# Moving the last block's transposes from crossbar DMA to TensorE, and ordering the last down group by column halves

## The chip, the cores and the metric

The kernel runs on one core of a Trainium2 chip. The metric is the device time of one execution in microseconds (us). Executions of the same kernel here agree within about 0.5%. The stage called "turn" below repeats to about 0.03 us between kernels that have the same instructions there (4.29 to 4.32 us), the "tail" only to about 0.2 us (3.53 to 3.77 us).

In profile lines, PE is TensorE's matmuls and PEld its weight loads, ACT is ScalarE, DVE is VectorE, and SPq is the queue that issues DMAs. A crossbar DMA is here a DMA with `transpose=True`, which transposes on the way.

## The reference, cut to what matters

A state-space convolution with a residual gives `h` (2048 rows of 640). Then a gated MLP is added to it:

```python
g = jnp.einsum("bsd,df->bsf", x, w_gate)      # x = layernorm(h), 640 -> 1728
u = jnp.einsum("bsd,df->bsf", x, w_up)
h = _sigmoid(g) * u
return jnp.einsum("bsf,fd->bsd", h, w_down)   # 1728 -> 640
```

## The kernel before

It works on four blocks of 512 rows. For each block, `prep` writes the normalized rows `ln2`, `turn` transposes them into `lnT`, the gate/up part makes `hm` and the down part multiplies `hm` with `Wd`. Since 1728 is 13 x 128 + 64, the last contraction step has only 64 rows; its matmuls are called half-height. A block's down part has two groups (`lp` = 0 and 2) of two 128-row sets (`k` = 0, 1). The next block's `prep` and `turn` are placed inside the down part of the present one. `DT` says per block whether `turn` uses the crossbar DMA; before, only the last block does.

```python
"DT": (0, 0, 0, 1)
# ... cut ...
def turn(b):
    ln2 = lns[b]
    lnT = lnTs[b] = xp.tile([P, 5, 4, 128], BF16, name="lnT", tag="G")
    if AT["DT"][b]:
        for i in range(4):
            nc.sync.dma_start(lnT[:, :, i, :], ln2[:, i, :], transpose=True)
        return
    # ... cut ...
    for dc in range(5):
        pt = psg_p.tile([P, 4, 128], BF16, name="ml_pt", tag="ml_pg")      # two buffers, shared with the gate
        for i in range(4):
            nc.tensor.transpose(pt[:, i, :], ln2[:, i, 128 * dc:128 * dc + 128], ident[:])
        if dc % 2 or b:
            nc.scalar.copy(lnT[:, dc], pt[:])
        else:
            nc.vector.tensor_copy(lnT[:, dc], pt[:])
# ... cut: gate/up ...
for lp in (0, 2):
    po = [[t[:, c] for c in range(2)] for t in (pso_p.tile([P, 2, 512], F32, name="ml_po", tag="ml_po") for _ in range(2))]

    def chunks(k, start, stop):
        lr = lp + k
        for ft in range(FT):                      # FT = 13
            for c in range(2):                    # column halves of 320
                nc.tensor.matmul(po[k][c][:, 0:320], lhsT=hm[:, ft, 128 * lr:128 * lr + 128], rhs=Wd[:, ft, 320 * c:320 * c + 320],
                                 start=(start and ft == 0), stop=(stop and ft == FT - 1))

    if not lp and b < NB - 1:
        prep(b + 1)
    chunks(0, True, False)
    if lp and b < NB - 1:
        turn(b + 1)
    # ... cut: four half-height matmuls, first k = 0 then k = 1 of each column half ...
    chunks(1, False, True)
    for k in range(2):
        # ... cut ...
        for c in range(2):
            if b < NB - 1:
                tb = Wd[:, 14 + k, 320 * c:320 * c + 320]
                nc.scalar.copy(tb, po[k][c][:, 0:320])
            nc.vector.tensor_tensor(h2[:, c], tb if b < NB - 1 else po[k][c][:, 0:320], h2[:, c], ALU.add)
        if b == NB - 1:
            nc.sync.dma_start(oh[b, :, lr:lr + 1, :], hs[b][:, lr:lr + 1, :])
```

## Time and profile before

| | before |
|---|---|
| median of 3 runs | 356.66 us (356.56 to 356.86) |
| span of the profiled run | 355.0 us |
| TensorE busy | 320.4 us, 90% |
| first half-height matmul of the last turn to the first gate matmul of block 3 | 302.71 to 307.01: 4.30 us |
| that gate to the first add after the last matmul | 307.01 to 351.44: 44.43 us |
| that add to the end of the span | 351.44 to 355.0: 3.56 us |

The last three rows cut the end of the kernel into the turn, the stretch that nothing in the change touches, and the tail. Their borders are start times in the timeline. The lines behind them stand in the prediction.

### The profile page before, as it was taken

How to read it: one execution, taken by the hardware profiler on the slowest of the kernel's cores; microseconds unless marked ns; L12 is line 12 of the kernel's file. 1: busy time of each engine (PE TensorE's matmuls, PEld its weight loads, DVE VectorE, ACT ScalarE, POOL GpSimd, SP SyncE). 2: the span in 40 equal slices, each digit the busy share in tenths (PEclk: the TensorE clock that was granted, in tenths of full speed). 3: DMA queues.
4: the chain of work that ended last, by engine and by line, in shares of the span. 5: the costliest groups of instructions: out<-in, count | busy, mean ns of one | idle time of the engine just before them, and what ended most of it. 6: DMA issues, size and time to landing. Idle time of an engine off the chain costs nothing.

```text
span 355.0 us, 6617 instructions
## 1 busy us (share of the span) xinstructions
PE 320.4 (90%) x2584; PEld 204.0 (57%) x2584; DVE 283.3 (80%) x570; ACT 245.9 (69%) x455; POOL 11.4 (3%) x20
## 2 busy tenths in 40 slices
PE   2587989997799999899999899998899999999995
PEld 1464667765487778755456554555554456544463
DVE  3899999999898799879999899999899951211222
ACT  6999999998999764673767845547844678455500
POOL 1020002200000000100000100000100001000000
PEclk9998999999999999999999999999999999999999
DMA  6990000454205339989500053000012000400011
GB/s 172 323 404 4 15 2 2 113 179 157 76 3 160 137 88 352 289 273 280 227 4 0 5 179 113 3 0 0 3 74 76 0 1 11 133 7 1 0 37 38
DMA packets 32391, 35.00 MB, mean 99 GB/s; under 512 B 19676, under 2 KB 27741, under 8 KB 32104
## 3 DMA queue, kind: packets, MB, share of 16 engines
q1 hardware_dynamic: 32360, 34.59, 30.7%
q8 instruction: 20, 0.33, 0.4%
q14 instruction: 11, 0.09, 0.1%
HBM read 24.70 MB, written 9.21 MB: 96 GB/s over the span
## 4 chain that ended last, share of the span: by engine, by line
DVE 28%; PE 18%; issue 14%; ACT 2%; POOL 1%; POOLq 0%; DVEq 0%; ACTq 0%
DVE u L694 5%; PE ml_po L942 5%; DVE u L693 5%; PE ml_pg L909 5%; PE ml_pu L909 4%; DVE u L696 3%; DVE u L697 3%; DVE ml_hm L920 2%; DVE VR L704 2%; PE ps_y L565 1%; DVE Z L673 1%; DVE y L701 1%; DVE y L702 1%; DVE h L805 1%; ACT ln L859 1%
## 5 line engine op out<-in xcount | busy, mean ns | idle before, releaser
L909 PE MATMUL ml_pg<-lnT,Wg 128*128 128x512 bf16 x260 | 64.6, 379 | 0.2 <-ACT ml_sg L917 0.2
L909 PE MATMUL ml_pu<-lnT,Wu 128*128 128x512 bf16 x260 | 64.4, 379 | 0.0
L942 PE MATMUL ml_po<-Wd,ml_hm 128*128 128x320 bf16 x416 | 59.5, 299 | 1.7 <-ACT Wd L963 1.7
L942 PEld LDWEIGHTS <-ml_hm 128*128 128x128 bf16 x416 | 40.1, 98 | 19.6 <-issue 3.7
L917 ACT ACTIVATE ml_sg<-ml_pg 128x512 bf16<-128x512 f32 x52 | 30.9, 597 | 25.5 <-PE ml_pg L909 11.9
L920 DVE TENSOR_TENSOR ml_hm<-ml_ub,ml_sg 128x512 bf16<-128x512 bf16 x52 | 22.0, 423 | 28.0 <-ACT ml_ub L919 28.0
L909 PEld LDWEIGHTS <-Wu 128*128 128x128 bf16 x260 | 25.4, 98 | 30.7 <-issue 0.3
L919 ACT CAST ml_ub<-ml_pu 128x512 bf16<-128x512 f32 x52 | 30.4, 584 | 17.0 <-PE ml_pu L909 16.9
L909 PEld LDWEIGHTS <-Wg 128*128 128x128 bf16 x260 | 25.4, 98 | 28.8 <-issue 0.4
L457 PE MATMUL ps_z<-u,c_G 128*128 128x320 bf16 x192 | 30.3, 307 | 4.5 <-ACT zs L458 2.7
L518 PE MATMUL ps_xk<-kv,c_KM 128*128 128x160 bf16 x320 | 27.0, 232 | 1.8 <-ACT S L522 0.8
L693 DVE TENSOR_TENSOR u<-Z,S 128x1280 bf16<-128x1280 bf16 x34 | 27.8, 820 | 0.0
L694 DVE TENSOR_TENSOR u<-Z,S 128x1280 bf16<-128x1280 bf16 x34 | 27.8, 820 | 0.0
L457 PEld LDWEIGHTS <-c_G 128*128 128x128 bf16 x192 | 18.9, 99 | 13.7 <-issue 6.0
L518 PEld LDWEIGHTS <-c_KM 128*128 128x128 bf16 x320 | 23.5, 98 | 4.5 <-issue 3.5
L247 PE MATMUL ps_t<-fr,c_dg 128*128 128x160 f16 (+1 forms) x180 | 19.7, 240 | 4.9 <-DMA c_dg<-s4c_dg 4.1
L247 PEld LDWEIGHTS <-c_dg 128*128 128x128 f16 x180 | 14.9, 100 | 11.4 <-DMA c_dg<-s4c_dg 4.7
L697 DVE TENSOR_TENSOR u<-u,u 128x1280 bf16<-128x1280 bf16 x23 | 18.9, 821 | 0.1
L696 DVE TENSOR_TENSOR u<-u,u 128x1280 bf16<-128x1280 bf16 x23 | 18.9, 821 | 0.0
L476 PE MATMUL pk<-tabB,tabA 128*128 128x84 bf16 x320 | 16.1, 200 | 1.8 <-ACT kts L477 1.4
L477 ACT CAST kts<-pk 128x420 bf16<-128x420 f32 x32 | 15.9, 558 | 1.8 <-PE pk L476 1.8
L476 PEld LDWEIGHTS <-tabA 128*128 128x128 bf16 x320 | 14.3, 97 | 4.8 <-issue 3.3
(158 smaller groups left out, 546.1 us busy)
## 6 DMA issues: line engine op xcount, KB each, us to landing
dz<-zs SPq DMA_DIRECT2D x12, 320.0 KB, 2.4
c_KM<-s4c_KM SPq DMA_DIRECT2D x1, 2560.0 KB, 12.6
dxk<-xk SPq DMA_DIRECT2D x16, 160.0 KB, 3.8
h<-in_A_u_dram SPq DMA_DIRECT2D x4, 640.0 KB, 4.4
eo<-dz SPq DMA_DIRECT2D x4, 640.0 KB, 4.3
S<-dxk SPq DMA_DIRECT2D x4, 640.0 KB, 5.3
Wg<-in_B_w_gate_dram SPq DMA_DIRECT2D x4, 520.0 KB, 9.4
Wu<-in_B_w_up_dram SPq DMA_DIRECT2D x4, 520.0 KB, 8.5
```

The source lines that it names most:

```text
L247: MM(ps[:, a, q * w:q * w + w], lhsT=dg[:, dk, :], rhs=fr[:, src, i, o + oo:o + oo + w], start=False, stop=(q == m - 1 and i == 1))
L457: MM(ps[:, ri, 0:UH], lhsT=G[:, ft, 0 if b in EO else hf, ri, r, :], rhs=us[b][:, r, o:o + UH], start=(r == rr[0]), stop=(r == rr[-1]))
L476: MM(pk[:, i, :], lhsT=A[:, ri, g].rearrange("p e c -> p (e c)"), rhs=B[:, ri, :, 4 * g:4 * g + 4], start=(ri == 0), stop=(ri == 1))
L518: mm = MM(ps[:, hf, ri * W:ri * W + W], lhsT=KM[:, ft, hf, ri, KI[d] + q, :], rhs=kv[:, j, :], start=(q == 0), stop=(q == len(KD[d]) - 1)).ins
L693: V(t1, z, k[:, :, :, hs_], ALU.mult)
L694: V(t2, z, k[:, :, ::-1, hs_], ALU.mult)
L696: V(s1, s1, t1, ALU.add)
L697: V(s2, s2, t2, ALU.add)
L909: nc.tensor.matmul(ps[:], lhsT=W[:, dc, f0:f0 + 128], rhs=lnT[:, dc].rearrange("p a b -> p (a b)"), start=(dc == 0), stop=(dc == 4))
L917: nc.scalar.activation(sg[:], pg[:], AF.Sigmoid)
L919: nc.scalar.copy(ub[:], pu[:])
L942: nc.tensor.matmul(po[k][c][:, 0:320], lhsT=hm[:, ft, 128 * lr:128 * lr + 128], rhs=Wd[:, ft, 320 * c:320 * c + 320], start=(start and ft ...
```

## The change

The intent: use the same transposes for every block, with no DMA on the way from `ln2` to `lnT`, and let the first column half of the very last row set be added and stored while TensorE still works on the second.

```diff
-      "DT": (0, 0, 0, 1)
+      "DT": (0, 0, 0, 0)
...
+            end = b == NB - 1 and lp
+
             def chunks(k, start, stop):
                 lr = lp + k
-                for ft in range(FT):
-                    for c in range(2):
-                        nc.tensor.matmul(po[k][c][:, 0:320], ...
+                for ft, c in [(ft, c) for c in range(2) for ft in range(FT)] if end and k else [(ft, c) for ft in range(FT) for c in range(2)]:
+                    nc.tensor.matmul(po[k][c][:, 0:320], ...
...
                     nc.vector.tensor_tensor(h2[:, c], ...)
-                if b == NB - 1:
+                    if end and k:
+                        nc.sync.dma_start(oh[b, :, lr, 320 * c:320 * c + 320], hv[:, 320 * c:320 * c + 320])
+                if b == NB - 1 and not (end and k):
                     nc.sync.dma_start(oh[b, :, lr:lr + 1, :], hs[b][:, lr:lr + 1, :])
```

Cut from the diff: `last_up`, which only gives the last gate/up step a name, and a setting `PW == 2`, which is not in use (`PW` is 0).

## The prediction

> **What bounds the kernel now.** The kernel works on four blocks of 512 rows. Each block's gated MLP has a gate/up part (matmuls `ml_pg`, `ml_pu`) and a down part (`ml_po`), and between two blocks the normalized rows `ln` have to be transposed into `lnT`. I read the page's busy times first, to see which engine could be the bound, then the chain that ended last, to see whether it really is.
>
> ```profile
> PE 320.4 (90%) x2584; PEld 204.0 (57%) x2584; DVE 283.3 (80%) x570; ACT 245.9 (69%) x455; POOL 11.4 (3%) x20
> ...
> DVE 28%; PE 18%; issue 14%; ACT 2%; POOL 1%; POOLq 0%; DVEq 0%; ACTq 0%
> ```
>
> TensorE is busy 90% of the span. The chain's shares name DVE for the early stages, but the change does not reach those. In order of time the chain is PE alone from 303.54 us to 351.42 us: the second half of the last down group of block 2, all of block 3's gate/up, and its down groups. So every microsecond of TensorE work added just before 303.5 us goes straight into the end, and so does every microsecond gained after the last matmul. I therefore read two places from the timeline: the turn from block 2 to block 3, and the tail. Blocks 0 to 2 are not touched: the built programs have the same VectorE order throughout, and on TensorE the only difference in order before the tail is 20 transposes put into the last turn.
>
> The turn from block 2 to block 3 (start us, duration us, engine, line, what):
>
> ```profile
> 299.07 3.35 ACT L859 ACTIVATE ln<-h,nmr,rstd 128x640 bf16<-128x640 bf16 x4 [0.95 <-DVE nmr L425]
> 300.02 5.28 SPq L868 DMA_TRANSPOSE lnT<-ln  x4
> 302.33 0.72 ACT L963 CAST Wd<-ml_po 128x320 bf16<-128x320 f32 x2
> 302.71 0.10 PEld L953 LDWEIGHTS <-ml_hm 64*128 64x128 bf16 x2 [0.26 <-issue]
> 302.71 0.82 PE L953 MATMUL ml_po<-Wd,ml_hm 64*128 64x320 bf16 x4
> ...
> 303.47 3.71 PE L942 MATMUL ml_po<-Wd,ml_hm 128*128 128x320 bf16 x26
> ...
> 307.01 1.24 PE L909 MATMUL ml_pg<-lnT,Wg 128*128 128x512 bf16 x5
> ```
>
> The four crossbar transposes are issued between 300.02 and 305.30 us and land 2.6 us after issue (median of the list of DMA issues), the last one, issued at 304.0, at about 304.0 + 2.6 = 306.6. TensorE reaches the first gate matmul at 307.01, straight from its down matmuls. The DMA transposes are therefore hidden already, with about 0.4 us to spare: taking them away gives nothing back. One small hole is there: the four half-height matmuls (L953) take 302.71 to 303.47 = 0.76 us, where the same four take 0.38 us in the chain at 339.84. The second pair waits because ACT, busy with the four `ln` rows, has evicted that buffer only by 303.05. So 0.38 us of waiting can be filled.
>
> The turn from block 1 to block 2 already uses TensorE transposes, and is thus a ready-made measurement of the new turn:
>
> ```profile
> 249.97 3.69 PE L942 MATMUL ml_po<-Wd,ml_hm 128*128 128x320 bf16 x26 [0.87 <-ACT Wd L963]
> ...
> 253.50 0.50 PE L881 MATMUL ml_pt<-c_ident,ln 128*128 128x128 bf16 x3
> ...
> 254.58 0.45 PE L881 MATMUL ml_pt<-c_ident,ln 128*128 128x128 bf16 x5 [0.58 <-ACT ln L859]
> ...
> 254.97 0.55 PE L953 MATMUL ml_po<-Wd,ml_hm 64*128 64x320 bf16 x3
> 255.06 1.63 ACT L883 COPY lnT<-ml_pt 128x512 bf16<-128x512 bf16 x3
> ...
> 255.68 0.38 PE L881 MATMUL ml_pt<-c_ident,ln 128*128 128x128 bf16 x4 [0.17 <-ACT lnT L883]
> ...
> 256.97 3.42 PE L942 MATMUL ml_po<-Wd,ml_hm 128*128 128x320 bf16 x24
> ...
> 260.23 1.24 PE L909 MATMUL ml_pg<-lnT,Wg 128*128 128x512 bf16 x5
> ```
>
> **What the Trainium skill says.** "VectorE: DVE Perf Modes", section "The three transpose paths", gives 390 ns for a 128x128 bf16 transpose on TensorE and 1309 ns by DMA. The trace has 219 ns from start to end for one on TensorE, so the measured value is shorter, and 1270 ns per DMA issue, which itself carries five 128x128 tiles. Neither is the figure needed: what a transpose takes from the other matmuls is its spacing. For that "TensorE: Matmul & The Clock Gate", section "Back-to-back issue gap", gives about 81 ns per load-and-multiply pair of 128 columns. The trace agrees: five transposes between 254.58 and 254.97 are 78 ns each (those at 256.74 to 256.97 only 58 ns). On the tail, "PSUM — Partial Sum Buffer", section "PSUM bank collisions raise a hardware error", says that a bank is guarded as a whole, and banks are independent; the two column halves lie in different banks, so the hardware would allow the overlap that the second part of the change wants. Whether the program uses it is another matter, below.
>
> **Part 1, the turn: remove 4 DMA transposes, add 20 TensorE transposes and 5 ACT copies.** Removed from the path: 0 (hidden, above). Added on TensorE: 20 x about 70 ns, between the two spacings, = 1.4 us. Filled in return: the first 8 transposes run from 302.71 to about 303.3, where TensorE had waited 0.38 us, and ACT's eviction is done by then. New waits: five `ml_pt` tiles share the two buffers of the gate tiles, so transposes of the third tile wait for ACT's copy of the first, those of the fourth for the second; the trace of the earlier turn shows 0.17 us for the first of these, and of the others some 0.1 together. Sum: 1.4 - 0.38 + 0.27 = 1.3 us.
>
> As a check, lay the earlier turn over this one. There the first copy of `lnT` starts at 255.06 and the first gate matmul at 260.23: 5.17 us. Here the last of the four `ln` rows is written by 302.42, before TensorE is free at 302.71, so the 0.58 us wait for `ln` of the earlier turn does not recur; the first tile's four transposes are issued by 302.71 + 4 x 0.078 = 303.02, less one spacing plus 0.22 us latency is 303.16, ACT is free at 303.05, so the copy starts at about 303.2. The gate then starts at 303.2 + 5.17 = 308.37, against 307.01: +1.36 us. (Comparing the turns whole, 10.26 against 7.88 us from first matmul of that down group to gate, would say +2.4, but that holds the wait for `ln`, which here falls away.) The two ways give 1.3 and 1.36. ACT's five copies of 589 ns (2.9 us) lie in time where ACT is idle anyway: 3.00 us before 307.21.
>
> **Part 2, the tail.** Meant: with the first column half finished 13 matmuls (13 x 0.14 = 1.8 us) earlier, its add and its store run under the other half, and after the last matmul there is one add instead of two. In the profile:
>
> ```profile
> 351.44 0.89 DVE L964 TENSOR_TENSOR h<-ml_po,h 128x320 bf16<-128x320 f32 x2 [2.75 <-PE ml_po L942]
> 352.36 0.33 SPq L966 DMA_DIRECT2D out_dram<-h  x1
> ```
>
> One add costs 0.40 us of the pair's 0.89 (they overlap by 0.09), so the intent would be worth 0.40 us, perhaps more with a smaller store. But in the changed program, as built, the matmuls of that accumulator signal only once, after the last of both halves, and the first half's add waits for exactly that count; the second half's add has no wait of its own, which it would need if the first had waited for less. Both halves are views of one two-bank tile, and the wait is kept per tile. So both adds still start after the last matmul. What does change: the first half's store is issued between the two adds, at about 352.0, the second at about 352.4 as before, each of 80 KB rather than one of 160 KB. I count 0 to -0.1 us.
>
> **Sum.** 356.66 + 1.3 - 0.05 = 357.9 us, 0.35% slower.
>
> **Rivals.** (a) The DMA transposes delayed something that the trace hides, so that removing them pays: the gate's first matmul stands 0.4 us after the landing, and no wait on that DMA is shown at 307.01. Against it. If so, 356.7 to 357. (b) The column halves work after all: against it, the signal counts of the built program. Worth -0.40, so 357.5. (c) The copy chain on ACT stretches the turn like the earlier ones: +2.4 us, 359; for it, ACT does ln, evictions and copies in one queue; against it, ln is ready 0.3 us before TensorE here. (d) Two stores of 640-byte rows land later than one of 1280-byte rows because both contend at the very end: +0.1 to +0.3 us. Nothing in the trace rules it out. (e) The transposes fit into gaps wholly: +0; against it, only 0.38 us of gap exist there.
>
> **Range and chances.** The turn is between +1.0 (all at 58 ns, no new wait) and +1.7 (all at 81 ns, waits doubled), the tail between -0.4 and +0.2, the runs before spread over 0.3 us. Range 357.2 to 358.5. A move by 2% is 7 us; no part reaches that. Within 2%: 0.98, the rest 0.01 each.
>
> **What would show it.** Right: in the new trace the first gate matmul of block 3 stands 1.1 to 1.6 us later than 307.01, 20 transposes start at about 302.7, the wait in L953 is gone; the stretch from that gate to the last matmul is unchanged at 44.4 us; both final adds come after the last matmul, back to back, with two stores. Wrong: a final add of 0.49 us before the last matmul ends (then b), a gate start at or before 307.3 (then a or e) or after 308.9 (then c), or a longer time from last add to end (then d).

## The result, and the profile after

Ratios here and below are the mean time of one kernel's runs over that of the other's of the same rounds, so they are not quite the ratio of the medians quoted beside them.

The changed kernel took 358.06 us (median of 4, 357.03 to 358.19) against 356.62 us: ratio 1.0033, 95% interval 1.0014 to 1.0052. It is slower by about a third of a per cent, inside the predicted range of 357.2 to 358.5, and within 2%.

The page of the changed kernel, busy times (engine, us, share of the span, instructions):

```profile
PE 322.3 (90%) x2604; PEld 206.0 (58%) x2604; DVE 283.3 (80%) x570; ACT 248.4 (70%) x460; POOL 11.4 (3%) x20
```

TensorE has exactly 20 more matmuls and ACT five more copies; VectorE is the same to the instruction.

The turn from block 2 to block 3 in the timeline of the changed kernel (start us, duration us, engine, line, what):

```profile
302.58 0.61 PE L882 MATMUL ml_pt<-c_ident,ln 128*128 128x128 bf16 x8
...
303.01 1.64 ACT L884 COPY lnT<-ml_pt 128x512 bf16<-128x512 bf16 x3
...
303.13 0.44 PE L962 MATMUL ml_po<-Wd,ml_hm 64*128 64x320 bf16 x3
...
303.64 0.38 PE L882 MATMUL ml_pt<-c_ident,ln 128*128 128x128 bf16 x4
...
303.96 0.31 PE L962 MATMUL ml_po<-Wd,ml_hm 64*128 64x320 bf16 x1
...
304.20 0.31 PE L951 MATMUL ml_po<-Wd,ml_hm 128*128 128x320 bf16 x1
...
304.34 0.39 PE L882 MATMUL ml_pt<-c_ident,ln 128*128 128x128 bf16 x4
...
304.57 0.30 PE L951 MATMUL ml_po<-Wd,ml_hm 128*128 128x320 bf16 x1
...
304.70 0.39 PE L882 MATMUL ml_pt<-c_ident,ln 128*128 128x128 bf16 x4
...
304.93 3.42 PE L951 MATMUL ml_po<-Wd,ml_hm 128*128 128x320 bf16 x24
...
308.19 1.24 PE L910 MATMUL ml_pg<-lnT,Wg 128*128 128x512 bf16 x5
```

The duration of a row with several matmuls contains the latency of the last one, 0.22 us for a transpose. The first eight transposes thus stand (0.61 - 0.22) / 7 = 56 ns apart, and the rows of four give the same within 3 ns: 20 x 56 ns = 1.12 us. The first row ends its issue at 302.58 + 8 x 0.056 = 303.03, but the half-height matmuls start at 303.13, and 0.10 us pass again before the one at 303.96: this is a hand-over to half-height matmuls. The kernel before has one such hand-over, and it lies before 302.71. A fair start for both kernels is therefore the last of the 52 down matmuls before the turn, first in the kernel before, then in the changed one:

```profile
302.48 0.30 PE L942 MATMUL ml_po<-Wd,ml_hm 128*128 128x320 bf16 x1
```

```profile
302.45 0.30 PE L951 MATMUL ml_po<-Wd,ml_hm 128*128 128x320 bf16 x1
```

From there to the gate it is 307.01 - 302.48 = 4.53 us before and 308.19 - 302.45 = 5.74 us now: the turn costs 1.21 us more. (From TensorE's first instruction of the turn it would be 5.61 against 4.30, 1.31 us, of which 0.10 is the hand-over that this border leaves out in the kernel before.)

The transposes start where the 0.38 us hole was, so the hole is filled. One wait is new. The weight load of the third tile's transposes starts at 303.50, right behind the three half-height matmuls, but its first matmul only at 303.64:

```profile
303.50 0.35 PEld L882 LDWEIGHTS <-ln 128*128 128x128 bf16 x4 [0.26 <-issue]
```

After other half-height matmuls the two start together (both at 303.47 in the kernel before), so this is a wait of 0.14 us. The chain of the changed kernel says what ended it (start us, length us, what):

```profile
303.03 0.57 ACT lnT L884
303.60 0.04 issue
303.64 0.38 PE ml_pt L882 x4
```

It is ACT's copy of the first tile, which gives its buffer free for the third. The other new cost is the fourth half-height matmul, alone now. Three cost 303.50 - 303.13 = 0.37 us, as much as four together (0.38), because they start in pairs: single starts in the packed trace are 347.323, 347.327, 347.469 and 347.472 for four in the kernel before. The one left alone takes 304.20 - 303.96 = 0.24 us, of which 0.23 is extra. The sum is 1.12 (transposes) + 0.10 (second hand-over) - 0.38 (hole) + 0.23 (lone matmul) + 0.14 (wait) = 1.21 us, the measured difference.

The tail of the changed kernel:

```profile
348.88 3.70 PE L951 MATMUL ml_po<-Wd,ml_hm 128*128 128x320 bf16 x26
...
352.62 0.89 DVE L973 TENSOR_TENSOR h<-ml_po,h 128x320 bf16<-128x320 f32 x2 [2.75 <-PE ml_po L951]
353.14 0.81 SPq L975 DMA_DIRECT2D out_dram<-h  x2
```

Both adds of the last row set start after the last matmul, one behind the other, as before; VectorE sat idle for 2.75 us while one half had long been finished. From gate to adds it is 352.62 - 308.19 = 44.43 us, unchanged, and from the adds to the end of the span 356.2 - 352.62 = 3.58 us against 3.56. In the packed trace these 26 matmuls raise their semaphore once, with the last one at 352.28; the first add waits for it, and the second has no wait on TensorE.

### The profile page after: what moved, and what is told of

It reads as the page before. It is cut to its first block, busy times and chain, and to the rows that moved or that the text cites. A ratio compares the mean times of both kernels' runs of the same rounds, so it can differ in the third digit from the quotient of the medians.

```text
span 356.2 us, 6655 instructions
## 1 busy us (share of the span) xinstructions
PE 322.3 (90%) x2604; PEld 206.0 (58%) x2604; DVE 283.3 (80%) x570; ACT 248.4 (70%) x460; POOL 11.4 (3%) x20
## 4 chain that ended last, share of the span: by engine, by line
DVE 26%; PE 16%; issue 14%; SPq 3%; DMA 2%; ACT 1%; POOL 1%; POOLq 0%; DVEq 0%; ACTq 0%
DVE u L694 5%; PE ml_po L951 5%; DVE u L693 5%; PE ml_pg L910 5%; PE ml_pu L910 4%; DVE u L696 3%; DVE u L697 3%; DVE ml_hm L931 2%; DMA Wl<-in_B_w_gate_dram 2%; DVE VR L704 2%; SPq L822 1%; SPq L823 1%; DVE Z L673 1%; DVE y L701 1%; DVE y L702 1%
```

## The experiments

Ten kernels were run, each with five rounds beside the kernel before on the same chip. The "turn" column is the time from TensorE's first instruction after the 52 down matmuls (a transpose or a half-height matmul) to the first gate matmul of block 3, the "tail" column from the start of the last row set's add (the last one, where the two are apart) to the end of the span, both from the profiled run. Where the turn begins with a transpose (changed kernel, e1, e5, e6), the column holds 0.10 us of hand-over that it leaves out elsewhere, as explained above; from the last of the 52 down matmuls the turn is 5.74 us in the first three and 6.68 in e6, against 4.53 in the kernel before.

| run | median us | before us | ratio, 95% interval | turn | tail |
|---|---|---|---|---|---|
| changed kernel | 358.06 | 356.62 | 1.0033 (1.0014 to 1.0052) | 5.61 | 3.58 |
| e1_turn_only | 358.42 | 356.87 | 1.0043 (1.0030 to 1.0056) | 5.61 | 3.77 |
| e2_tail_only | 356.70 | 356.87 | 1.0000 (0.9987 to 1.0014) | 4.29 | 3.59 |
| e3_tail_split | 356.13 | 356.87 | 0.9979 (0.9966 to 0.9992) | 4.29 | 3.00 |
| e4_no_turn | 357.33 | 356.87 | 1.0010 (0.9995 to 1.0026) | 4.30 | 3.76 |
| e5_after_split | 357.32 | 356.83 | 1.0017 (1.0005 to 1.0030) | 5.60 | 3.08 |
| e6_twice | 359.00 | 356.83 | 1.0063 (1.0051 to 1.0076) | 6.55 | 3.62 |
| e7_xbar_123 | 359.38 | 356.83 | 1.0075 (1.0061 to 1.0088) | 4.32 | 3.53 |
| e8_split_dve | 355.93 | 356.83 | 0.9975 (0.9963 to 0.9988) | 4.04 | 3.08 |
| e9_xbar_23 | 357.13 | 356.40 | 1.0023 (1.0007 to 1.0040) | 4.29 | 3.74 |
| e11_xbar_23_split_dve | 356.70 | 356.40 | 1.0005 (0.9986 to 1.0023) | 3.99 | 3.15 |

Why the two last columns are better evidence than the medians: the same point of the program, the last of the 52 down matmuls before the turn, starts at 302.48 us before, 302.45 in the changed kernel, 302.96 in e1 and 301.84 in e3, although nothing earlier differs in instruction order between these kernels. About 1 us of spread thus comes from earlier stages and is not due to the change. Why the earlier stages vary was not examined.

### The two parts alone

e1_turn_only is the kernel before with one edit:

```diff
-      "DT": (0, 0, 0, 1)
+      "DT": (0, 0, 0, 0)
```

> Kernel before with only the transposes of the last turn moved to TensorE; tail as before. Theory (the turn is the whole cost, the tail split does nothing): +1.2 to +1.4 us over before, first gate matmul of block 3 at about 308.2 us. Rival (the split pays 0.4 us and the turn therefore costs more): +1.6 to +1.8 us.

Measured: +0.43%, that is 1.5 us, with an interval of 1.1 to 2.0 us. The median alone cannot part theory and rival, since the interval covers both. The stage can: the turn is 5.61 us, the same as in the whole change, and from the last down matmul 5.74 us, 1.21 more than before. The gate stood at 308.70, not 308.2, because this run reached the turn 0.5 us late; its tail, with instructions as before, took 0.2 us more.

e2_tail_only is the changed kernel with `DT` set back to `(0, 0, 0, 1)`.

> Kernel before with only the tail of the change (matmuls of the last group by column halves, two stores); crossbar transposes kept. Theory (both adds wait for one signal after the last matmul): within 0.1 us of before, both adds back to back after the last matmul. Rival 1 (the halves overlap): -0.4 us. Rival 2 (two small stores land later than one): +0.1 to +0.3 us.

Measured: ratio 1.0000, tail 3.59 against 3.56 us. Its two adds start at 351.31 us, back to back, after VectorE has sat idle for the same 2.75 us as in the changed kernel. The theory holds: no overlap is there. No later landing of the two small stores is seen either; with two stores the tail is 3.58, 3.59 and 3.62 us (changed kernel, e2, e6), with one 3.53 to 3.77 (before, e1, e4, e7, e9), so an effect well below 0.2 us stays possible.

### Is it the tile that keeps the halves together?

e3_tail_split is e2_tail_only with the accumulators of the last row set taken as two tiles:

```diff
             end = b == NB - 1 and lp
+            if end:
+                po[1] = [psg_p.tile([P, 512], F32, name="ml_po", tag="ml_pg") for _ in range(2)]
```

> As the tail alone, but the two column halves of the last group are two tiles of one bank each, taken from the gate tiles' pool, which is free by then. Theory (the wait is kept per tile): the first half's add runs about 1.8 us before the last matmul ends, one add of 0.49 us is left after it, -0.4 us against before. Rival (the end is set by something else, such as the landing of the last store): within 0.1 us of before.

Measured: 0.9979, interval 0.9966 to 0.9992. The end of its timeline:

```profile
349.03 0.49 DVE L975 TENSOR_TENSOR h<-ml_po,h 128x320 bf16<-128x320 f32 x1 [0.99 <-PE ml_po L953]
...
350.80 0.49 DVE L975 TENSOR_TENSOR h<-ml_po,h 128x320 bf16<-128x320 f32 x1 [1.27 <-PE ml_po L953]
```

The first half's add now runs 350.80 - 349.03 = 1.77 us ahead of the other, under the matmuls. The tail is 3.00 us against 3.59 in e2, which has the same matmul order and the same stores; only the tiles differ. The packed trace has the semaphore raised twice now, 13 matmuls apart (348.69 and 350.46), and each add waits for its own. So the wait kept per tile is what made the second part of the change do nothing. Of the 0.59 us, 0.40 is the add. The rest would be the last store, now alone at the end and of half the size; it ended 2.5 us after its issue (350.80 + 0.52 to 353.8) against 2.64 before (352.36 to 355.0), but stores vary by as much from run to run.

e5_after_split puts the same two lines into the changed kernel.

> The changed kernel with the last group's two column halves as two one-bank tiles, so that the split works. Theory (the two parts are independent): +1.3 us from the turn and -0.4 to -0.6 us from the tail, +0.7 to +0.9 us over before; from the last matmul to the end of the span about 3.0 us, where before has 3.56. Rival (the gain of the tail came from the lucky runs of the earlier experiment): +1.2 us or more.

Measured: ratio 1.0017, that is +0.6 us with an interval of +0.2 to +1.1; turn 5.60, tail 3.08 us. The parts add up: +1.21 - 0.48 = +0.73 us by stages.

### What the crossbar transposes cost before

e4_no_turn leaves out the last turn; its output is wrong (relative error 0.71).

```diff
     def turn(b):
+        if b == 3:
+            lnTs[b] = lnTs[2]
+            return
         ln2 = lns[b]
```

> Kernel before without any transposes in the last turn: block 3 reads block 2's transposed rows, so its output is wrong on purpose. Measures what the crossbar transposes cost in all. Theory (they are hidden): within 0.1 us of before, first gate matmul still at about 307.0 us. Rival (they hold the gate, or slow other work): faster by 0.3 us or more.

Measured: the turn takes 4.30 us, the same as with the crossbar transposes to the hundredth. The gate stood at 306.41, not 307.0, because the turn began 0.6 us earlier in that run. In time it is not faster (1.0010, interval 0.9995 to 1.0026). The crossbar transposes cost nothing where they were, which settles rival (a) of the prediction.

### Is the turn's cost TensorE time or the chain of copies?

e6_twice does every transpose of the last turn twice, into the same place:

```diff
-            for i in range(4):
+            for i in (0, 1, 2, 3) * (2 if b == 3 else 1):
                 nc.tensor.transpose(pt[:, i, :], ...)
```

> The changed kernel with each of the 20 transposes of the last turn done twice into the same place (the result stays right), ACT's copies as they are. Theory (the turn's cost is TensorE's own time at 58 to 80 ns a transpose, with some 0.3 us of waiting for ACT's copies that can be filled): from the first half-height matmul's earliest time to the gate 1.0 to 1.4 us longer than the 5.61 us of the changed kernel, so +2.3 to +2.8 us over before. Rival (the turn's cost is the chain of ACT copies through two buffers, not TensorE's time): less than 0.4 us more than the changed kernel.

Measured: the turn grew from 5.61 to 6.55 us, +0.94, a little under the expected 1.0 to 1.4; in time +2.2 us over before, just under the expected 2.3. The timeline says why:

```profile
302.70 1.06 PE L882 MATMUL ml_pt<-c_ident,ln 128*128 128x128 bf16 x16
303.69 0.31 PE L962 MATMUL ml_po<-Wd,ml_hm 64*128 64x320 bf16 x2
303.99 1.09 PE L882 MATMUL ml_pt<-c_ident,ln 128*128 128x128 bf16 x16
305.01 0.31 PE L962 MATMUL ml_po<-Wd,ml_hm 64*128 64x320 bf16 x2
305.27 0.61 PE L882 MATMUL ml_pt<-c_ident,ln 128*128 128x128 bf16 x8
305.71 3.69 PE L951 MATMUL ml_po<-Wd,ml_hm 128*128 128x320 bf16 x26
```

Sixteen transposes stand (1.06 - 0.22) / 15 = 56 ns apart. Twenty more at 56 ns are 1.12 us; 0.94 was paid. The rest was saved at the half-height matmuls, which the scheduler placed two and two here and not three and one: with the waits behind them they take 0.30 + 0.26 us (from 303.69 and 305.01), against 0.51 + 0.24 in the changed kernel. The rival, that the copies alone set the turn, would have let the second set of transposes run almost free, and it falls: more than four fifths of the added TensorE time show. Because the placement changed too, the split is not exact.

### The opposite change

If a turn by TensorE costs 1.2 us, should not all turns go by DMA? e7_xbar_123 has `DT` of `(0, 1, 1, 1)`.

> The opposite change: crossbar DMA for all three later turns, none by TensorE except the first. The scheduler also moves some VectorE work. Theory (TensorE is the bound from block 1 on, the transposes and their waits cost it about 1.3 us a turn, the DMA lands about 7.5 us after the first ln row begins, just in time): -1.0 to -2.6 us against before. Rival (VectorE, 98% busy from 206 to 260 us, is the bound there, or transposes at the head of the in-order DMA queue hold the loads behind them): within 0.5 us of before, or slower.

Measured: slower by 0.75%. The theory fell. The turn from block 0 to 1 did shorten, from the first matmul of its second down group to the gate 205.80 - 196.17 = 9.63 us against 206.12 - 195.80 = 10.32. But TensorE then waited for VectorE, in two views of its waits (206 to 262 us, then 262 to 305 us; who waited for whom, us in total, times, longest):

```profile
PE ml_po L953 <- DVE ml_hm L931: 2.0, 1, 2.0
PE ml_po L942 <- DVE ml_hm L920: 0.9, 1, 0.9
```

```profile
PE ps_y L801 <- DVE VR L787: 1.2, 1, 1.2
```

The first kind was there before too, with 1.4 us; the others were not. The scheduler had also changed VectorE's order, so this run mixes two things. e9_xbar_23, `DT` of `(0, 0, 1, 1)`, keeps blocks 0 and 1 as they were up to the turn.

> Crossbar DMA for the last two turns, TensorE for the first two; the scheduler reorders about twenty VectorE instructions in block 1's down part and block 2, fewer than when all three turns change. Theory (VectorE, not the transposes' place, made the all-crossbar kernel slow: VectorE is 98% busy from 206 to 260 us, so TensorE time won in the turn from block 1 to block 2 comes back as waits on VectorE): the turn itself shortens by 1 us or more, but waits on VectorE in block 2 return at least half; the whole between -0.7 and +1.0 us. Rival (TensorE is the bound from block 2 on): -1.0 to -1.5 us.

Measured: slower by 0.23% (0.07 to 0.40%), about 0.8 us, inside what the theory allowed and against the rival. Where it went shows in the timeline. The turn from block 1 to 2 and the end of block 2's gate/up in e9:

```profile
249.43 3.69 PE L942 MATMUL ml_po<-Wd,ml_hm 128*128 128x320 bf16 x26 [0.87 <-ACT Wd L963]
...
258.57 1.24 PE L909 MATMUL ml_pg<-lnT,Wg 128*128 128x512 bf16 x4
```

```profile
284.94 0.43 PE L801 MATMUL ps_y<-VR,c_IV 128*128 128x320 bf16 x2 [0.92 <-DVE VR L787]
...
290.07 1.24 PE L926 MATMUL ml_pg<-lnT,Wl 128*128 128x512 bf16 x5
```

The same in the kernel before, for the second border (its first is in the prediction):

```profile
290.46 1.24 PE L926 MATMUL ml_pg<-lnT,Wl 128*128 128x512 bf16 x5
```

The turn fell from 260.23 - 249.97 = 10.26 us to 258.57 - 249.43 = 9.14: 1.12 us won. From that gate to the last gate/up step it then took 290.07 - 258.57 = 31.50 us against 290.46 - 260.23 = 30.23: 1.27 us given back, 0.92 of it in one wait for VectorE. So the TensorE time won in this turn did not reach the end. The profiled run is e9's fastest (356.69 us), so the 0.8 us by which the medians are slower cannot be found in this trace and stay unexplained. Whether the give-back is VectorE's amount of work or its new order is open: the schedule cannot be held fixed while `DT` is changed.

### A version that beats both

e8_split_dve has the crossbar transposes of before, the working split, and this, for block 2's first down group:

```diff
-                    if b < NB - 1:
+                    direct = b == NB - 1 or b == NB - 2 and not lp and k
+                    if not direct:
                         tb = ...
                         nc.scalar.copy(tb, po[k][c][:, 0:320])
-                    nc.vector.tensor_tensor(h2[:, c], tb if b < NB - 1 else po[k][c][:, 0:320], h2[:, c], ALU.add)
+                    nc.vector.tensor_tensor(h2[:, c], po[k][c][:, 0:320] if direct else tb, h2[:, c], ALU.add)
```

> Kernel before with the working tail split and, in block 2's first down group, VectorE adding the second row group straight from PSUM instead of waiting for ACT's eviction behind the ln rows. Theory: the 0.38 us hole before the last turn's half-height matmuls goes, as far as the landing of the crossbar transposes allows (about 0.4 us of slack there), so -0.3 us more than the tail split's -0.4 to -0.6, in all -0.7 to -1.0 us. Rival (the landing comes first): the gate waits for the DMA and the gain is that of the tail split alone.

Measured: 355.93 us, ratio 0.9975 (0.9963 to 0.9988), about 0.9 us faster than before. Its turn:

```profile
302.35 0.45 PE L964 MATMUL ml_po<-Wd,ml_hm 64*128 64x320 bf16 x4
302.73 3.71 PE L953 MATMUL ml_po<-Wd,ml_hm 128*128 128x320 bf16 x26
306.39 1.24 PE L910 MATMUL ml_pg<-lnT,Wg 128*128 128x512 bf16 x5
```

The four half-height matmuls take 0.38 us, the hole is gone. But the 26 matmuls to the gate take 306.39 - 302.73 = 3.66 us, where before they took 307.01 - 303.47 = 3.54: of the 0.38 us gained 0.12 went again, so 0.26 was won. The last crossbar transpose was issued at about 303.7. The views list no wait on its landing, but the packed trace has one: TensorE's sequencer waits until the landing at 306.30, the gate's weight load follows at 306.36, and the gate stands 0.09 us after the landing, although TensorE would have been free at 306.27 (its last down matmul at 306.135, plus 0.136). In the kernel before the landing came at 306.66, so the gate could have stood at 306.75; the slack was 0.26 us, not the 0.4 us of the prediction, and e8 used it up. Theory and rival are each right in part: the hole went, and then the landing set the gate.

e11_xbar_23_split_dve joins e8 and e9.

> The same with the working tail split and the eviction by VectorE in the last turn. Theory and rival as for the crossbar in the last two turns, plus -0.7 to -0.9 us each: theory -1.6 to +0.3 us, rival -1.7 to -2.4 us against before.

Measured: 1.0005 (0.9986 to 1.0023), inside the theory's range and outside the rival's. It gains about 0.2% on e9, where e8 gained 0.25% on before; it is no faster than before. e8 has the lowest ratio of all kernels tried, but the interval of e3, the split alone, overlaps it (0.9966 to 0.9992); that the direct add gives more rests on the turns of e8 and e11 (4.04 and 3.99 us against 4.30).

## Why the prediction was right

- **What is removed is worth 0.** Shown by e4: without any turn the stage is 4.30 us, as with the crossbar. The slack was 0.26 us and not 0.4 (see e8), which changes nothing here.
- **What is added on TensorE: foretold 1.4 us, measured 1.12 us.** The transposes stand 56 ns apart. The prediction took 78 ns from 254.58 to 254.97 in the earlier turn, but that distance contains a hand-over of 0.10 us to the half-height matmuls; the row itself, (0.45 - 0.22) / 4, gives 58 ns. So its sentence that the trace agrees with 81 ns is a misreading.
- **The hole of 0.38 us is filled.** It was: transposes start at once after the 52 matmuls, and the half-height matmuls no longer wait for ACT's eviction. Not foretold were the second hand-over (0.10 us) and the half-height matmul left alone (0.23 us).
- **New waits: foretold 0.27 us, measured 0.14 us.** It is the wait for the first copy, foretold with 0.17; the others did not show.
- **Sum of the turn: foretold 1.3 us, measured 1.21 us.** That the sum came so near is partly luck: 0.28 us too much for the transposes and 0.13 too much for waits made up for 0.33 us that were not foreseen. The check by laying the earlier turn over this one was sounder, since that turn contains all these pieces: from the first copy to the gate it foretold 5.17 us, and 308.19 - 303.01 = 5.18 us was measured. Its 1.36 us came out too high because the first copy started at 303.01 and not at 303.2.
- **The tail: foretold 0 to -0.1 us, measured +0.02 us**, which is within its scatter of 0.2 us. The reason given, one signal per tile, is shown by e3 and e5: with two tiles the tail is 3.00 to 3.15 us (e3, e5, e8, e11), about 0.5 less, of which 0.40 is the add.
- **Rivals.** (a) fell by e4, (b) by e2, (c) and (e) by the measured turn; for (d) no sign was found. In the medians the change costs 1.4 us (by the interval 0.5 to 1.9); 1.2 of it is the turn.

The one wrong expectation lies outside the prediction: in e7 what a turn costs in block 3 was carried over to the turns before blocks 1 and 2, where time won on TensorE did not reach the end.

## What to carry to other kernels

Ask of a transfer not how long it takes but whether anything waits for its landing: a slower path that is hidden beats a faster one that takes time from the engine that sets the end. Before work is overlapped by reordering it, look at what signals its completion: here an add on one view of a tile waited for the other view, and with two tiles it did not. And the worth of an engine's time is local: 1.2 us counted in full in the last turn, and the 1.1 us won one turn earlier did not show in the time.

## What the Trainium skill lacked or had wrong

- "VectorE: DVE Perf Modes", section "The three transpose paths", compares durations, 390 ns on TensorE and 1309 ns by DMA. The trace has 219 ns for one on TensorE, and 1270 ns on the issuing queue for five tiles together with 2.6 us to landing. What decided here is not in its table: 56 ns of TensorE time per transpose, from one start to the next, about 590 ns of ACT per copy of four, and 0 for the DMA when hidden.
- "TensorE: Matmul & The Clock Gate", section "Back-to-back issue gap", gives about 81 ns per load-and-multiply pair at 128 columns in a stream, and says that its formula for a single one, about 56 ns, counts too low there. The transposes, each with its own weight load, stood about 56 ns apart here in runs of 4, 8 and 16.
- No page was found that says that two column views of one PSUM tile share one completion signal in the built program, so that an add on a finished bank waits for the other bank: 2.75 us of VectorE idling before two adds, against 1.27 us and one add with two tiles.
